# Sliding-window attention and soft mixture of experts on one core: second-layer weight chunks of one expert, eight 128-column transposes, row sums in two parts, ten row blocks stored by column halves

## Chip, core and metric

The kernel runs on one core of one Trainium2 chip. The metric is device time in microseconds (us); smaller is better. A core has TensorE (PE, with its weight loads shown as PEld), VectorE (DVE), ScalarE (ACT), GpSimd (POOL), SyncE (SP) and 16 DMA engines.

## The reference

The input is q, k and v of shape (8, 8, 576, 64) in fp32, a router phi (512 x 32) and the weights of eight experts, w1 (8 x 512 x 1024) and w2 (8 x 1024 x 512). The output is 4608 x 512 in fp32.

```python
scores = scale * q @ k.T            # heads 0-3: window of 32; heads 4-7: 128, every fourth
x = softmax(masked scores) @ v      # (4608, 512) after the heads are put side by side
logits = x @ phi                    # 32 slots, 4 of each expert
d = softmax of logits over the rows (axis 0)
slot_input = (d.T @ x).reshape(8, 4, 512)
for e in range(8):
    slot_out[e] = np.maximum(slot_input[e] @ w1[e], 0.0) @ w2[e]
c = softmax of logits over the slots (axis 1)
out = c @ slot_out
```

## The kernel before

The program is written as operations with engine, cost and key. A planner (`Prog.schedule`) puts them in order by estimated due times, and `emit` writes each engine's list with its semaphore waits. POOL and SP operations keep the order in which they are written. Where the planner sees a gap on TensorE within `FILL`, it inserts matmuls of the identity that nobody reads (`filler`, L1014); the function `keep` (L910) puts in `WARM` more of them after part p2 below.

The first 130 us are eight units of attention. POOL loads each unit's q, v and k with a cast to bf16 into one of three parts of `stg`; TensorE transposes (L574, L579), makes scores (L617) and weighted values (L671); the logits are made in `expT` (L726, L731) and the slots' inputs accumulate (L774). The weights follow in the same POOL queue, cast to bf16 on the way: w1 of experts 0 to 6 into `WD`, then "w17" and the second-layer weights. Their order in the queue is w17, p3a, p0, p1, p2, p3b, p3c, p3d, p3e. A number in such a name is a pair of experts g, so p0 is w2 of experts 0 and 1, and pair 3 is cut into five parts by chunk and, for the last four, by column half. One chunk is 128 rows of w2, of both experts: in `(e p) c f` partitions 0 to 63 hold expert 2g and partitions 64 to 127 hold expert 2g + 1, sixteen chunks in all. p0 goes in 13 transfers, some of them small dummies into `scr` (`TURNS`)[...].

From 132 us on comes the tail, to which the change belongs:

1. The slots' inputs are transposed (`fold`, L827) into `siT`, and layer 1 runs (L846). ReLU puts the first half of the hidden values into `h_sb` on ACT (L854), the second on DVE (L857).
2. Because a chunk holds two experts, the hidden values are transposed with the selector `half` in two groups of 64 columns: 2 times 16 matmuls (L866). ACT and DVE copy the results into `hT` (L875), one instruction each.
3. Layer 2 multiplies `hT` with the chunks of p3a, p0, p1 (L894), then TensorE sums the 36 columns of the combine weights (L921; DVE's reciprocal at L926 gives `rtok`), then come p2, the `WARM` matmuls, p3b and p3c. With p3b and p3c the first 256 columns of the slots' outputs are complete, and DVE scales them into `so_sb` (L935). p3d and p3e give the other 256 columns.
4. The output is made in seven groups of row blocks of 128 rows, `TILES` with 1, 2, 3, 5, 4, 8 and 13 blocks. The first `NSPLIT` = 4 groups, eleven blocks, are made in two column halves: the first half (rows of 1 KB) while p3d and p3e are still on their way, the second after them. The last three groups, 25 blocks, are made with full rows. TensorE multiplies (L972), and DVE (L983 for two blocks of 256 columns at once, L991 for one) or ACT (L989) scales by `rtok` into a staging place that the weights no longer need (`STAGE`). SP stores each group, or half of a group, with one transfer (L1005) when it is complete.

Of the kernel before, what the change touches and what calls it, by code (L numbers as in the profile page):

```python
# [23 lines left out]
FILL = (118,141)  # L24
# [293 lines left out]
def bass_dilated_sliding_attn__then__soft_moe_slots_kernel(  # L318
# [14 lines left out]
    def sb(name, shape, dt=BF16):  # L333
        return A(nc.sbuf_tensor(name, shape, dt))

    WARM = 7
    TURNS = ((32, 0, 4), (32, 1, 4), (32, 2, 4), (16, 3, 8), (15, None, 0), (6, 39, 8), (2, None, 0),
             (2, 87, 8), (6, None, 0), (4, 103, 8), (2, 7, 8), (2, None, 0), (2, 23, 8))
    W2 = {"p3a": (3, 0, 4, 0, 512), "p0": (0, 0, 16, 0, 512), "p1": (1, 0, 16, 0, 512),
          "p2": (2, 0, 16, 0, 512), "p3b": (3, 4, 14, 0, 256), "p3c": (3, 14, 16, 0, 256),  # L340
          "p3d": (3, 4, 14, 256, 512), "p3e": (3, 14, 16, 256, 512)}
# [27 lines left out]
    half = sb("half", [128, 2, 32])  # L369
# [40 lines left out]
    b_psA, b_csum, b_rcs, b_rtok = [Buf() for _ in range(4)]  # L410
# [35 lines left out]
    def wload(name):  # L446
# [3 lines left out]
        if name[:2] == "w1":  # L450
            src = moe_w1[int(name[2:])].rearrange("(p c) f -> p c f", c=4)
            dst = ap.rearrange("p (c f) -> p c f", c=4)
        else:
            g, c0, c1, f0, f1 = W2[name]
            src = moe_w2[2 * g:2 * g + 2].rearrange("e (p c) f -> (e p) c f", c=16)[:, c0:c1, f0:f1]
            dst = ap.rearrange("p (c f) -> p c f", f=f1 - f0)
        if name == "p0":
            src = src.rearrange("p (x c) f -> p x (c f)", x=2)
            dst = ap.rearrange("p (x y) -> p x y", x=2)[:, :, 0:4096]

            def skewed(g):
                res = []
                for i, (n, r, step) in enumerate(TURNS):
                    if r is None:
                        res.append(g.dma_start(scr[0:n, i], src[0:n, :, 0:8]))
                    else:
                        e = r + step * (n - 1) + 1
                        res.append(g.dma_start(dst[r:e:step], src[r:e:step]))
                return res
            op("pool", skewed, after=b.prev, a=[b], cost=0.6 * (len(TURNS)), sem=sem, nbytes=512 * 8192,  # L470
               nd=288, nq=len(TURNS))
            return
# [6 lines left out]
    home(stg[:, 2, 4096:6144], [b_stg[2]], "p3a")  # L479
    home(stg[:, 2, 6144:8704], [b_stg[2]], "p3b")  # L480
# [52 lines left out]
    for x in range(2):  # L533
        for j in range(4):
            op("dve", lambda g, x=x, j=j: g.tensor_copy(
                half[32 * j:32 * j + 32, x, 8 * j + 4 * x:8 * j + 4 * x + 4],
                ident[32 * j:32 * j + 32, 32 * j + 4 * x:32 * j + 4 * x + 4]),
               r=[b_id], w=[b_half], cost=0.1, key=1)
# [321 lines left out]
    for p_ in range(2):  # L860
        ht = tile(psum, 1)

        def pe(t, p_=p_, ht=ht):
            for c in range(8):
                for x in range(2):
                    i_ = t.matmul(bank(ht)[64 * x:64 * x + 64, 32 * c:32 * c + 32],  # L866
                                  h_sb[:, 8 * p_ + c::16], half[:, x, :], start=True, stop=True)
            return i_
        op("pe", pe, r=[b_h[0], b_h[1], b_half], w=[ht], alloc=[ht], cost=0.95, mode="h",
                 key=K1, ni=32)  # L870

        def ev(en, p_=p_, ht=ht):
            d_ = hT[:, 8 * p_:8 * p_ + 8, :].rearrange("p c (j i) -> p c j i", j=4)[:, :, :, 0:8]
            s_ = bank(ht)[:, 0:256].rearrange("p (c j i) -> p c j i", c=8, j=4)
            return en.activation(d_, s_, ACTF.Copy) if p_ == 0 else en.tensor_copy(d_, s_)  # L875
        op("act" if p_ == 0 else "dve", ev, r=[ht], w=[b_hT[p_]], cost=0.35, key=K1)

    TILES = []
    NSPLIT = 4
    POOLS = False  # L880
    for n in (1, 2, 3, 5, 4, 8, 13):
# [5 lines left out]
    for k_, name in enumerate(W2):  # L887
        g, c0, c1, f0, f1 = W2[name]
        wv = HOME[name][0].rearrange("p (c f) -> p c f", f=f1 - f0)
        for h_ in range(f0 // 256, f1 // 256):  # L890
            def pe(t, k_=k_, name=name, g=g, c0=c0, c1=c1, h_=h_, wv=wv, f0=f0):
                for c in range(c0, c1):
# [3 lines left out]
                                  wv[:, c - c0 + (name == "p0" and c > 7), 256 * h_ - f0:256 * h_ - f0 + 256],  # L896
                                  start=(k_ == 0 and c < 4), stop=(k_ > 3 and c >= 12))
                return i_
            last_ = op("pe", pe, r=b_hT + [HOME[name][1]], alloc=[sp_] if k_ == h_ == 0 else [],
                       a=[sp_, b_sp[h_]], cost=0.13 * (c1 - c0) / 4, mode="c",  # L900
                       ni=2 * (c1 - c0),
                       key=K1 + 2 + 0.5 * k_ + 0.1 * h_ + (28 if k_ > 5 else 0))
            if k_ == 2:
                mid = last_
# [11 lines left out]
    rs = tile(psum, 1)  # L916

    def rsum(t):
        for o, (_, n) in enumerate(TILES):
            for j in range(n):  # L920
                i_ = t.matmul(bank(rs)[:, rcol[o] + j:rcol[o] + j + 1], tok[o][j], rowm[:],  # L921
                              start=True, stop=True)
        return i_
    op("pe", rsum, r=b_expT + [b_rowm], w=[rs], alloc=[rs], cost=2.0, key=K1 + 3, ni=72,
       after=[mid])
    op("dve", lambda vv: vv.reciprocal(rtok[:], bank(rs)[:, 0:N_TOK // 128]), r=[rs], w=[b_rtok],  # L926
       cost=0.2, key=K1 + 1)

# [10 lines left out]
    for o_ in P.ops[-2:]:  # L939
# [6 lines left out]
    STAGE = [(w17f[:, 0:512], ["w17"]), (w17f[:, 512:1536], ["w17"]), (p0f[:, 0:1536], ["p0"]),  # L946
             (p0f[:, 1536:4096], ["p0"]), (p1f[:, 0:2048], ["p1"]), (WDf[:, 6656:10752], wdh),
             (WDf[:, 0:6656], wdh)]
    nev = 0
    for o, h_ in [(o, h_) for h_ in range(2) for o in range(NSPLIT)] + [(o, None) for o in range(NSPLIT, 7)]:  # L950
        t0, n = TILES[o]
        ost = STAGE[o][0].rearrange("p (j f) -> p j f", j=n)
        sl = slice(0, 512) if h_ is None else slice(256 * h_, 256 * h_ + 256)
        ob = Buf()
        for x in STAGE[o][1]:
            ob.prev = ob.prev + HOME[x][1].ready + HOME[x][1].reads
        k1 = K1 + 30 + o + 10 * (2 if h_ is None else h_)
        w = sl.stop - sl.start
        for j0 in range(0, n, 2):
            po = tile(psum, w // 256)  # L960
            kk = k1 + 0.1 * j0
            b_po = [Buf(), Buf()]

            def slot(j, po=po, w=w):
                if w == 512:
                    return pair(po)[:, j, :]
                return bank(po)[:, w * j:w * j + w]
            m = min(2, n - j0)
            for js in [range(m)] if w == 256 else [(j,) for j in range(m)]:
                def pe(t, o=o, slot=slot, j0=j0, js=js, sl=sl):  # L970
                    for j in js:
                        i_ = t.matmul(slot(j), tok[o][j0 + j], so_sb[:, sl], start=True, stop=True,  # L972
                                      skip_group_check=True)
                    return i_
                j = js[0]
                p0 = op("pe", pe, r=(b_so if h_ is None else b_so[h_:h_ + 1]) + b_expT, a=[po],
                        w=[b_po[j]], alloc=[po] if j == 0 else [], after=[p0] if j else [],
                        cost=0.22 if h_ is None else 0.15 * m, key=kk + 0.01 * j, ni=2 * len(js))
                col = rcol[o] + j0 + j

                def ev(en, slot=slot, ost=ost, js=js, j0=j0, sl=sl, col=col, po=po):
                    if en is nc.vector and len(js) == 2:
                        return en.tensor_tensor(  # L983
                            ost[:, j0:j0 + 2, sl], bank(po).rearrange("p (j f) -> p j f", j=2),
                            rtok[:, col:col + 2].unsqueeze(2).to_broadcast([128, 2, 256]), AluOp.mult)
                    for j in js:
                        d_, s_, sc_ = ost[:, j0 + j, sl], slot(j), rtok[:, col + j - js[0]:col + j - js[0] + 1]
                        if en is nc.scalar:
                            i_ = en.activation(d_, s_, ACTF.Copy, scale=sc_)  # L989
                        else:  # L990
                            i_ = en.tensor_scalar(d_, s_, sc_, None, op0=AluOp.mult)  # L991
                    return i_
                if w == 256:
                    o_ = op(("dve", "act"), ev, r=[b_po[j], b_rtok], a=[ob], after=ob.prev,
                            cost={"dve": 0.7 if m == 2 else 0.48, "act": 0.47 * m}, key=kk)
                else:
                    o_ = op(("dve", "act")[nev % 2], ev, r=[b_po[j], b_rtok], a=[ob], after=ob.prev,
                            cost=0.66, key=kk)
                    nev += 1
                o_.touch.append(po)  # L1000
                po.left += 1
        so = DmaSem(nc, f"s_out{o}_{h_}")
        s_out.append(so)
        op("pool" if POOLS and h_ is not None and (h_ or o > 1) else "sp",
           lambda e, t0=t0, n=n, ost=ost, sl=sl: [e.dma_start(  # L1005
               out[t0:t0 + 128 * n, sl].rearrange("(p j) f -> p j f", j=n), ost[:, :, sl])],
           r=[ob], cost=0.1, sem=so, nbytes=512 * n * w, key=k1)
# [60 lines left out]
```

## Time and profile before

| what | value |
|---|---|
| median of five runs | 179.17 us (177.8 to 181.73) |
| the profiled execution | 178.26 us, its span 176.5 us |
| mean granted TensorE clock | 0.927 of full |
| busy: PE, DVE, ACT, POOL | 133.1, 113.4, 95.7, 43.5 us |
| POOL's queue (loads with cast) | 30.94 MB, 87.1% of 16 engines' span |
| SP's queue (output) | 9.50 MB, 13.8% |
| HBM read, written | 61.93 MB, 9.44 MB: 404 GB/s over the span |

The page cuts the span into 40 slices of 4.4 us; a digit is a busy share in tenths. A transfer's bytes are counted on the side that it writes, so loads that turn fp32 into bf16 count half of what they read. Busy time of an engine says little here: what counts is which wait ends last in a stage.

### The profile page before, as it was taken

How to read it: one execution, taken by the hardware profiler on the slowest of the kernel's cores; microseconds unless marked ns; L12 is line 12 of the kernel's file. 1: busy time of each engine (PE TensorE's matmuls, PEld its weight loads, DVE VectorE, ACT ScalarE, POOL GpSimd, SP SyncE). 2: the span in 40 equal slices, each digit the busy share in tenths (PEclk: the TensorE clock that was granted, in tenths of full speed). 3: DMA queues.
4: the chain of work that ended last, by engine and by line, in shares of the span. 5: the costliest groups of instructions: out<-in, count | busy, mean ns of one | idle time of the engine just before them, and what ended most of it. 6: DMA issues, size and time to landing. Idle time of an engine off the chain costs nothing.

```text
span 176.5 us, 5828 instructions
## 1 busy us (share of the span) xinstructions
PE 133.1 (75%) x2619; PEld 105.1 (60%) x2619; DVE 113.4 (64%) x259; ACT 95.7 (54%) x144; POOL 43.5 (25%) x83
## 2 busy tenths in 40 slices
PE   0009798695999877999949999986999998695000
PEld 0009587584897676898848978874646685441000
DVE  6850388965887984898974699899550102899000
ACT  2004889584895963878944689686310100797000
POOL 7991707007004302600100690106100000000000
PEclk9999999997899998899995799999999999999655
DMA  5999999999999999999999999999999999799996
GB/s 82 190 215 211 213 217 213 214 217 212 220 213 210 217 219 207 216 219 213 212 215 214 217 213 216 214 219 212 230 200 219 230 166 196 224 341 402 458 440 290
DMA packets 11672, 40.80 MB, mean 231 GB/s; under 512 B 2176, under 2 KB 8064, under 8 KB 8192
## 3 DMA queue, kind: packets, MB, share of 16 engines
q0 software_dynamic: 7744, 30.94, 87.1%
q1 hardware_dynamic: 3904, 9.50, 13.8%
q8 instruction: 20, 0.33, 0.7%
q14 instruction: 4, 0.03, 0.0%
HBM read 61.93 MB, written 9.44 MB: 404 GB/s over the span
## 4 chain that ended last, share of the span: by engine, by line
PE 37%; DMA 21%; DVE 20%; issue 6%; ACT 5%; POOL 3%; POOLq 1%; DVEq 0%
DMA TT<-in_moe_w_dram 16%; PE ps L579 9%; PE ps L574 6%; DMA stg<-in_k_dram 5%; DVE PT L632 5%; PE ps L671 4%; PE ps L642 4%; PE ps L617 4%; DVE WD L991 4%; DVE XB L682 4%; PE ps L726 4%; DVE VN L647 4%; PE ps L699 3%; ACT TT L599 2%; ACT PT L624 2%
## 5 line engine op out<-in xcount | busy, mean ns | idle before, releaser
L624 ACT ACTIVATE PT<-ps 128x768 bf16<-128x768 f32 x48 | 37.0, 816 | 11.1 <-PE ps L617 10.7
L599 ACT ACTIVATE TT<-ps 128x864 f32<-128x864 f32 x32 | 28.6, 896 | 20.1 <-PE ps L579 17.2
L682 DVE TENSOR_TENSOR XB<-ps,RV 96x768 bf16<-96x768 f32 x32 | 30.4, 951 | 0.9
L579 PE MATMUL ps<-ident,stg 96*64 96x96 bf16 x576 | 18.7, 232 | 14.4 <-DMA stg<-in_k_dram 12.9
L579 PEld LDWEIGHTS ps<-ident,stg 96*64 96x64 bf16 x576 | 16.7, 129 | 15.7 <-DMA stg<-in_k_dram 12.9
L647 DVE COPY VN<-ps 128x768 bf16<-128x768 bf16 x32 | 17.1, 543 | 12.0 <-PE ps L642 11.9
L617 PE MATMUL ps<-TT 64*128 64x96 bf16 x384 | 16.3, 211 | 6.5 <-issue 4.2
L671 PE MATMUL ps<-VN,PT 128*128 128x65 bf16 x384 | 18.7, 198 | 3.2 <-issue 2.0
L430 POOL DMA_DIRECT2D stg<-in_q_dram x16 | 8.8, 549 | 42.4 <-PE ps L579 23.7
L671 PEld LDWEIGHTS ps<-VN,PT 128*128 128x128 bf16 x384 | 15.4, 101 | 4.5 <-issue 2.1
L642 PE MATMUL ps<-ident,TT 128*128 128x128 bf16 x192 | 17.2, 234 | 0.6 <-ACT PT L624 0.3
L617 PEld LDWEIGHTS ps<-TT 64*128 64x128 bf16 x384 | 10.2, 97 | 10.4 <-issue 4.5
L712 ACT ACTIVATE XT<-ps 128x576 bf16<-128x576 bf16 x22 | 13.7, 652 | 3.8 <-PE ps L699 3.8
L574 PE MATMUL ps<-ident,stg 96*128 96x96 bf16 x288 | 14.7, 206 | 0.4 <-DVE XB L682 0.4
L699 PE MATMUL ps<-ident,XB 96*128 96x96 bf16 x192 | 13.6, 218 | 0.9 <-DVE XB L682 0.9
L574 PEld LDWEIGHTS ps<-ident,stg 96*128 96x128 bf16 x288 | 13.2, 98 | 1.3 <-DVE XB L682 0.5
L642 PEld LDWEIGHTS ps<-ident,TT 128*128 128x128 bf16 x192 | 12.2, 104 | 2.9 <-DVE VN L647 0.6
L632 DVE TENSOR_TENSOR PT<-PT,mask_d 128x768 bf16<-128x768 bf16 x24 | 12.9, 545 | 1.1 <-ACT PT L624 1.0
L632 DVE TENSOR_TENSOR PT<-PT,mask_p 128x768 bf16<-128x768 bf16 x24 | 12.8, 551 | 1.0 <-ACT PT L624 0.6
L699 PEld LDWEIGHTS ps<-ident,XB 96*128 96x128 bf16 x192 | 10.5, 106 | 2.3 <-DVE XB L682 1.2
L972 PE MATMUL ps<-so_sb,expT 128*128 128x512 bf16 (+1 forms) x47 | 9.6, 334 | 1.9 <-DVE so_sb L935 1.2
L989 ACT ACTIVATE stg<-ps,rtok 128x256 f32<-128x256 f32 (+1 forms) x12 | 5.1, 512 | 10.6 <-PE ps L972 10.6
(83 smaller groups left out, 184.6 us busy)
## 6 DMA issues: line engine op xcount, KB each, us to landing
WD<-in_moe_w_dram POOLq DMA_DIRECT2D x7, 1024.0 KB, 30.6
stg<-in_q_dram POOLq DMA_DIRECT2D x16, 288.0 KB, 20.3
stg<-in_v_dram POOLq DMA_DIRECT2D x16, 288.0 KB, 21.1
stg<-in_k_dram POOLq DMA_DIRECT2D x16, 288.0 KB, 22.2
out_dram<-WD SPq DMA_DIRECT2D x1, 3328.0 KB, 12.4
stg<-in_moe_w_dram POOLq DMA_DIRECT2D x4, 512.0 KB, 20.4
stg<-in_moe_w_dram POOLq DMA_DIRECT2D x1, 2048.0 KB, 21.9
TT<-in_moe_w_dram POOLq DMA_DIRECT2D x1, 2048.0 KB, 23.2
```

The lines of the kernel that those rows point to most:

```text
L574: i_ = t.transpose(bankb2(pt, a)[:, 96 * kk:96 * kk + 96], two[:, j // 2, c, :], ident[0:96, 0:96])
L579: i_ = t.transpose(bankb2(pt, a)[64 * hx:64 * hx + 64, 96 * kk:96 * kk + 96], src[:, hx, c, :], ident[0:96, 0:96])
L599: return ac.activation(d, sv, ACTF.Copy)
L617: i_ = t.matmul(pair(sc)[:, hx, QB * x:QB * x + QB], win(u, 1, h01, blk_, bpar)[64 * hx:64 * hx + 64], win(u, 0, h01, blk_, bpar)[64 * hx: ...
L624: op("act", lambda ac: ac.activation(sbt(pt)[:, 0:768].rearrange("p (x n) -> p x n", x=2), pair(sc)[:, :, 0:384], ACTF.Exp, scale=SCALE), ...
L632: return dv.tensor_tensor(p_, p_, m.unsqueeze(1).to_broadcast([128, 2, 384]), AluOp.mult)
L642: i_ = t.transpose(bankb(pv)[:, 128 * m:128 * m + 128], win(u, 2, h01, m, bpar), ident[:, :])
L647: op("dve", lambda dv: dv.tensor_copy(sbt(vn)[:, :, :, 0:64], bankb(pv)[:, 0:768].rearrange("p (m x d) -> p m x d", m=6, x=2)), r=[pv], w= ...
L671: i_ = t.matmul(pair(po)[:, bk, 65 * po_:65 * po_ + 65], sbt(pts[i])[:, o_:o_ + 128], sbt(vn)[:, m, half, 0:65], start=True, stop=True)
L682: op("dve", lambda dv: dv.tensor_tensor(sbt(xb)[:].rearrange("p m (x h d) -> p h x m d", x=2, h=2)[:, h01], pv()[:, :, :, 0:64], sbt(rv)[: ...
L699: i_ = t.transpose(bankb(px)[:, QB * m:QB * m + QB], sbt(xb)[:, m, 128 * x:128 * x + 128], ident[0:QB, 0:QB])
L712: return en.activation(d, s_, ACTF.Copy)
```

## The change

- A chunk of second-layer weights now holds 128 rows of one expert: chunks 0 to 7 belong to expert 2g and 8 to 15 to expert 2g + 1. A partition reads two runs of 16 KB, one from each expert, where it read one of 32 KB. `half` has 16 columns for each of the two slot sets instead of 32, and 8 matmuls of 128 weight columns stand in place of the 32 transposes. The copies into `hT` have two instructions each.
- p3a has chunks 0 to 5 (0 to 3 before), p3b and p3d have chunks 6 to 13 (4 to 13 before). p3b and p3d go in two transfers each, since their chunks come from two experts.
- The row sums and their reciprocals are in two parts: 10 columns after layer 1, 26 after p1.
- `TILES` is 1, 1, 2, 3, 3, 4, 8, 14 and `NSPLIT` is 5: ten blocks by column halves, 26 with full rows. The blocks of the first groups are taken in the units 1, 1, 2, 2, 2, 2, also across the border of two groups. DVE evicts two blocks with two instructions instead of one (L983 goes).
- `WARM` is 8 instead of 7, and `FILL` ends at 138 instead of 141 of the planner's time. In the order that results, the four filling matmuls just ahead of the transposes give way to the ten row sums. Ahead of that place every engine's order is the same as before.

```diff
-FILL = (118,141)
+FILL = (118,138)
-    WARM = 7
+    WARM = 8
-    W2 = {"p3a": (3, 0, 4, 0, 512), "p0": (0, 0, 16, 0, 512), "p1": (1, 0, 16, 0, 512),
-          "p2": (2, 0, 16, 0, 512), "p3b": (3, 4, 14, 0, 256), "p3c": (3, 14, 16, 0, 256),
-          "p3d": (3, 4, 14, 256, 512), "p3e": (3, 14, 16, 256, 512)}
+    W2 = {"p3a": (3, 0, 6, 0, 512), "p0": (0, 0, 16, 0, 512), "p1": (1, 0, 16, 0, 512),
+          "p2": (2, 0, 16, 0, 512), "p3b": (3, 6, 14, 0, 256), "p3c": (3, 14, 16, 0, 256),
+          "p3d": (3, 6, 14, 256, 512), "p3e": (3, 14, 16, 256, 512)}
...
-            src = moe_w2[2 * g:2 * g + 2].rearrange("e (p c) f -> (e p) c f", c=16)[:, c0:c1, f0:f1]
-            dst = ap.rearrange("p (c f) -> p c f", f=f1 - f0)
+            src = moe_w2[2 * g:2 * g + 2].rearrange("e (p c) f -> e p c f", c=8)
+            dst = ap.rearrange("p (c f) -> p c f", f=f1 - f0) if name != "p0" else None
+            if c1 - c0 < 16:
+                def rows(gp):
+                    res = []
+                    for x in range(2):
+                        lo, hi = max(c0, 8 * x), min(c1, 8 * x + 8)
+                        if lo < hi:
+                            res.append(gp.dma_start(dst[:, lo - c0:hi - c0, :],
+                                                    src[x][:, lo - 8 * x:hi - 8 * x, f0:f1]))
+                    return res
...
+            src = src.rearrange("e p c f -> p e (c f)")
+            dst = ap.rearrange("p (x y) -> p x y", x=2)[:, :, 0:4096]
...
-            for c in range(8):
-                for x in range(2):
-                    i_ = t.matmul(bank(ht)[64 * x:64 * x + 64, 32 * c:32 * c + 32],
-                                  h_sb[:, 8 * p_ + c::16], half[:, x, :], start=True, stop=True)
+            for c in range(4):
+                i_ = t.matmul(bank(ht)[:, 32 * c:32 * c + 32], h_sb[:, 4 * p_ + c::8],
+                              half[:].rearrange("p x i -> p (x i)"), start=True, stop=True)
...
-    NSPLIT = 4
-    POOLS = False
-    for n in (1, 2, 3, 5, 4, 8, 13):
+    NSPLIT = 5
+    for n in (1, 1, 2, 3, 3, 4, 8, 14):
...
+    row_sums(0, [ffn1])
+    row_sums(1, [mid])
+
+    def scaled(en, d_, s_, c):
+        if en is nc.scalar:
+            return en.activation(d_, s_, ACTF.Copy, scale=rtok[:, c:c + 1])
+        return en.tensor_scalar(d_, s_, rtok[:, c:c + 1], None, op0=AluOp.mult)
...
+        for us in [units[0:1], units[1:2]] + [units[i:i + 2] for i in range(2, len(units), 2)]:
...
-                    if en is nc.vector and len(js) == 2:
-                        return en.tensor_tensor(
-                            ost[:, j0:j0 + 2, sl], bank(po).rearrange("p (j f) -> p j f", j=2),
-                            rtok[:, col:col + 2].unsqueeze(2).to_broadcast([128, 2, 256]), AluOp.mult)
```

The other lines of the diff carry this through: the column sums' buffers `b_rt`, the function `store` with SP's transfers, and the staging places `STAGE` for eight groups.

## The prediction

> **What bounds the kernel now.** I read the page's rows by slice first. The DMA share stands at 9 from the second slice to the end, with one dip. The granted clock is full from 99.7 us to 164.5 us, and the matmul rows are empty after 161.6 us. So the span is a transfer time: weights and inputs in, then 9.44 MB of output out.
>
> ```profile
> span 176.5 us, 5828 instructions
> ...
> DMA  5999999999999999999999999999999999799996
> ```
>
> Next I cut the last 35 us into windows of one transfer kind each (columns: busy us of PE, PE loads, DVE, ACT, POOL, then clock, DMA share, GB/s; an in-transfer counts its bf16 side, so 215 GB/s is 430 read).
>
> ```profile
> 104.00:109.00 5.00, 5.00 (x114) 4.65 (x112) 4.60 (x12) 4.17 (x8) 1.99 (x4) 1.00 1.01 211
> 134.00:141.00 7.00, 7.00 (x103) 3.96 (x103) 0.98 (x2) 0.98 (x2) 0.00 (x0) 1.00 1.02 218
> 142.00:149.00 7.00, 6.87 (x159) 5.09 (x151) 0.44 (x2) 0.00 (x0) 0.00 (x0) 1.00 1.41 193
> 149.60:151.10 1.50, 1.36 (x15) 1.05 (x17) 1.29 (x3) 1.07 (x3) 0.00 (x0) 1.00 0.78 100
> 151.10:152.10 1.00, 0.70 (x12) 0.22 (x11) 0.83 (x3) 0.86 (x3) 0.00 (x0) 1.00 0.41 135
> 152.10:153.10 1.00, 0.47 (x5) 0.43 (x6) 0.62 (x2) 0.00 (x0) 0.00 (x0) 1.00 0.96 321
> 153.00:159.00 6.00, 5.50 (x28) 2.81 (x25) 6.00 (x11) 5.83 (x12) 0.00 (x0) 1.00 1.01 340
> ```
>
> The reader is to see the one hole, from 149.6 to 153 us, between the last weights (p3d, p3e) and an output stream that runs without a break from 153 us on. Weighing 149.6 to 151.1 against the 1.41 share of small-row loads and the rest against 1.0, the hole is worth 0.67 + 0.59 + 0.04 = 1.3 us. Outside it the end can move only if bytes become cheaper.
>
> What opens the hole is read from the timeline and the store issues:
>
> ```profile
> 139.05 2.10 PE L866 MATMUL ps<-half,h_sb 128*64 128x32 bf16 x32
> 143.91 1.91 PE L921 MATMUL ps<-rowm,expT 128*128 128x1 bf16 x36
> 146.74 1.69 PE L910 MATMUL ps<-mask_p,ident 128*128 128x512 bf16 x7
> 148.35 0.51 PE L894 MATMUL ps<-stg,hT 128*32 128x256 bf16 x10
> 148.95 0.48 DVE L935 TENSOR_SCALAR so_sb<-ps,rcs 128x256 bf16<-128x256 f32 x1 [2.71 <-PE ps L894]
> ...
> 150.32 0.35 SPq L1005 DMA_DIRECT2D out_dram<-stg  x1
> 150.89 0.61 SPq L1005 DMA_DIRECT2D out_dram<-stg  x1
> 151.62 0.54 SPq L1005 DMA_DIRECT2D out_dram<-stg  x1
> 152.26 0.59 SPq L1005 DMA_DIRECT2D out_dram<-stg  x1
> ```
>
> Landings are issue plus the issue table's time: p2 120.49 + 23.2 = 143.7, p3b 121.03 + 26.0 = 147.0, p3c 121.99 + 25.7 = 147.7, p3d 151.0, p3e 151.7 us. So p3c was in at 147.7, but TensorE reached p3b only at 148.35, when its seven warming matmuls ended: the first half is 0.65 us late for TensorE's own reasons. The second half waits for nothing but p3e:
>
> ```profile
> 123.64 28.07 DMA TT<-in_moe_w_dram
> 151.72 0.04 issue
> 151.76 0.30 PE ps L894 x2
> ```
>
> **The change, part by part.**
>
> *Transposes.* 32 (L866) took 2.10 us, a pitch of 63 ns. No row has the new shape. The nearest are the 36 row sums, also with 128-column strided weights: 1.91/36 = 53 ns. Bounds 53 and 100 ns (a 128x128 load in L574 lasts 98, if none overlapped); I take 60, close to the nearest row: 8 x 60 = 0.5 us, 1.6 us less. Each eviction becomes two pieces of 64 elements for one of 256 (383 ns ACT, 425 ns DVE). The shortest row like it, 128x128 cast, is 291 ns; two pieces cost 0.4 to 0.58, I take 0.5. The DVE one now starts at about 139.7 and ends at 140.2 instead of 141.6 us, so hT is ready 1.4 us sooner.
>
> *Row sums.* 10 columns go into the wait for the DVE's relu (TensorE only filled there, 138.08 to 139.04): 0.53 us, hidden; without cover it would delay the transposes by that. 26 stay after p1, 1.4 us for 1.9.
>
> *Weights.* p3a grows from 4 to 6 chunks of 512 columns and heads the queue of p0, p1, p2; p3b and p3d shrink from 10 to 8. p2 (16 such chunks) followed p1 (landed 112.04 + 21.9 = 133.9) by 9.8 us, 0.61 per chunk, so p2 lands 1.2 us later, at 144.9. Ten quarter-size chunks of p3d took 151.0 - 147.7 = 3.3 us, 0.33 each. Four fewer small ones save 1.32 and cost 1.22: p3e gains 0.1. Against that, p1 and p2 go in 8 KB packets from two experts for 16 KB ones; w1 is loaded in 8 KB packets: 211 against 218 GB/s above. Over 5 us this ratio is rough, because whole packets are counted at their end; the packet records have 605 ns for 8 KB and 1,227 for 16 KB, equal per byte. Ends: -0.1 and +0.6 us (3% of the 19.5 us of p1 and p2); I take +0.1, by the packet times. Two more POOL issues (0.6 to 1.0 us each) end near 126 us, 16 us before their data moves. So p3e stays at 151.7; p3c, with two small chunks fewer behind it, lands at 148.3.
>
> Here a rule speaks against the change. The Trainium skill, *DMA: Bandwidth & Descriptors*, section "Latency and other measured facts", gives copies whose row pitch is a large power of two as slow: 207 GB/s at 512 KiB and 164 at 2 MiB, where full is 214. The two runs of a partition now lie one expert apart, 1024 x 512 x 4 B = 2 MiB. By the rule's worst figure p0, p1 and p2, some 29 us, would take 214/164, 8.8 us more. The row says otherwise: before, half of the partitions already read the one expert and half the other in the same transfer, and it is the fastest window (218). I take no loss, and keep the rule's milder end (3%, 1 us) for a rival.
>
> *TensorE after that.* Layer-2 parts p3a, p0, p1: 76 matmuls at the 30 ns of L894 (2.15/72) from 140.4 to 142.7; 26 row sums to 144.1; wait for p2 (144.9) and its 32 to 146.0; eight warming matmuls at 0.24 (1.69/7) to 147.9; p3b (landed 147.7) to 148.2; p3c at 148.35. Before, p3e's landing led to so_sb in 0.37 us, so so_sb starts at 148.7 instead of 148.95: **0.27 us sooner, of the 1.6 saved**. The rest is swallowed by p2 and p3c. What is late next is p3c.
>
> *First stores.* Tile 1 has one block, not two, so its store can go when ACT is done (480 ns) and SP free: issues at about 150.05, 150.45 instead of 150.32, 150.89, and 0.35 us long instead of 0.61. Packets start 0.8 us after a small issue: the second store's data follow the first's without the gap that 151.1 to 152.1 shows. Against this DVE evicts pairs in two instructions, 2 x 0.44 for 0.60 (L983 starts at 150.25 and 150.85): the third store can't leave before 150.9, the fourth 151.8; a gap of 0.3 to 0.4 us stays. Counting blocks out by 154.25 (0.38 us each), I get 7.4 for 6.7: 0.27 us gained; ends 0 and 0.9 (the hole nearly shut). Later DVE is no bound: after 20 half blocks and 26 full ones it ends at 163.8, as before (163.6), 4 us ahead of the stream.
>
> *Ten rows by columns instead of eleven.* One block goes out once at 2 KB a row, not twice at 1 KB. The last store's 13 blocks took (163.66 + 12.4) - (159.10 + 9.1) = 7.9 us, 0.605 each; ten half blocks of the second half landed from 156.9 to 160.8, 0.38 to 0.39 each. Saved 2 x 0.385 - 0.605 = 0.16 us. Two more stores cost SP 0.7 us, beside a full queue.
>
> *Clock.* The Trainium skill, *TensorE: Matmul & The Clock Gate*, section "Why this matters for your kernels", wants no idle gap above about 3 us. The trace is stricter: 3.41 us windows with 1.52 and 1.19 us of matmul were followed by half clock, 1.97 and 2.17 were not. The rule lets the new gaps (1 us at most) pass; by the row they are near the edge, as the tail's windows fall from 2.17 to about 2.0. If it trips, pairs cost 0.87 instead of 0.66 us for one window: 0.9 us, hidden by the same 4 us.
>
> **Sum:** -0.27 - 0.16 = **-0.4 us**. The profiled execution took 178.26 us (1.76 around its span): 177.85. The median of the runs is 179.17, 0.5% above it; on that scale 178.7.
>
> **Rivals.**
> 1. *Hidden anyway*: the store pipeline sets the hole; an earlier first half leaves the same gaps. For: stores are issued one after another. Against: the second issue waited for ACT. Only the cheaper rows count: -0.16, 179.0 us. Chance 0.17.
> 2. *The hole shuts*: -0.9 - 0.16: 178.1 us. Against: the slower DVE pair. Chance 0.1.
> 3. *Slower: the two-expert reads of p0, p1 and p2.* Place: 113 to 144 us. At 3% 29 us become 30, so +0.9 - 0.3 = +0.6, 179.8; at the rule's 2 MiB figure +8.4, 187.6. It decides from 1.5% (0.4 us). Against: the 218 window. Chance 0.13.
> 4. *p2 arrives too late for the warming matmuls.* From 0.65 us later than reckoned the first half starts later than now: +0.2, 179.4. Chance 0.08.
>
> The forecast has 0.52. About 1% is what a measurement here can tell, since the five runs shown spread over 2%. All but the strong end of rival 3 lie inside that; with the spread of medians I give 0.11 faster, 0.76 within, 0.13 slower. The range takes in rival 2 with a low median (177.2) and rival 3's mild end with a high one (180.7).
>
> **What would show it.** Right: transposes near 0.5 us, so_sb's first half near 148.7, p3e still near 151.7, a second store within 0.5 us of the first, last store issued near 163.9. Wrong: p3e after 152.3 (rival 3), warming matmuls ending after p3c lands (rival 4), or an unbroken DMA share from 151 us (rival 2).

## The result: 0.46% slower, where 0.2% faster was forecast

| | before | changed |
|---|---|---|
| median of all runs | 178.88 us (80 runs) | 178.98 us (43 runs) |
| lower and upper quartile | 177.72, 179.96 | 178.66, 179.60 |
| fastest run | 176.94 | 177.62 |
| ratio, 95% interval | | 1.0046 (1.0027 to 1.0065) |
| span of the profiled execution | 176.5 | 176.9 |

The ratio compares the runs of each kernel within 1.5% of its fastest, which leaves out 27 of the 80 runs of before and 5 of the 43 of the changed kernel. The medians of all runs differ by 0.1 us only. The quartiles say why: the change raises the lower quartile by 0.9 us and takes 0.4 us from the upper one.

The page of the changed kernel, rows by slice, and below them the clock row of before:

```profile
span 176.9 us, 5780 instructions
...
PEclk9999999997899998799996999999999987999655
DMA  5999999999999999999999999999999999699997
```

```profile
PEclk9999999997899998899995799999999999999655
```

Two things are new in the tail. The DMA dip in the sixth slice from the end is deeper (6 for 7), and the granted clock falls in slices 33 and 34 (8, 7), ahead of that dip. Cut as before, the hole reads (columns as in the prediction):

```profile
149.60:151.10 1.50, 1.01 (x10) 0.93 (x10) 1.12 (x3) 0.58 (x2) 0.00 (x0) 1.00 0.66 85
151.10:152.10 1.00, 0.72 (x13) 0.22 (x10) 1.00 (x4) 1.00 (x4) 0.00 (x0) 1.00 0.32 109
152.10:153.10 1.00, 0.19 (x2) 0.18 (x3) 0.75 (x2) 0.42 (x2) 0.00 (x0) 1.00 0.50 167
```

By the prediction's weighing it is 0.80 + 0.68 + 0.50 = 2.0 us, where 1.3 were lost before and 1.0 expected. The timeline of the same execution says why (line 908 is layer 2, 925 the warming matmuls, 937 so_sb):

```profile
140.88 1.62 PE L977 MATMUL ps<-rowm,expT 128*128 128x1 bf16 x26
142.54 0.32 DVE L981 RECIPROCAL rtok<-ps 128x26 f32<-128x26 f32 x1 [4.14 <-PE ps L977]
144.83 1.90 PE L908 MATMUL ps<-TT,hT 128*32 128x256 bf16 x32 [2.33 <-DMA TT<-in_moe_w_dram]
146.66 2.41 PE L925 MATMUL ps<-mask_p,ident 128*128 128x512 bf16 x8
149.00 0.40 PE L908 MATMUL ps<-stg,hT 128*32 128x256 bf16 x8
149.54 0.48 DVE L937 TENSOR_SCALAR so_sb<-ps,rcs 128x256 bf16<-128x256 f32 x1 [6.68 <-PE ps L908]
```

TensorE comes to p2 early and waits 2.33 us. p2's 32 matmuls then take 1.90 us and the eight warming ones 2.41, where 1.06 and 1.89 to 1.90 are their times at full clock (a_warm and a_pad below). p3b starts at 149.0, with p3c in since 148.1, and so_sb at 149.54 instead of the forecast 148.7. The windows view, cut at the clock's own steps, shows the cause:

```profile
140.91:144.32 3.41, 1.59 (x28) 1.51 (x26) 0.32 (x1) 0.00 (x0) 0.00 (x0) 1.00 1.04 192
144.32:147.73 3.41, 2.90 (x35) 1.51 (x36) 0.00 (x0) 0.00 (x0) 0.00 (x0) 0.50 1.44 194
```

A window with 1.59 us of matmul (first number after its length) is followed by one at clock 0.50 (the third number from the end). The chain of waits no longer goes from p3e into the output, but from p2:

```profile
118.88 25.91 DMA TT<-in_moe_w_dram
144.83 1.90 PE ps L908 x16
146.72 2.34 PE ps L925 x8
150.41 2.05 DVE stg L990 x5
```

**One number carries every profile.** Span minus the start of so_sb's first half is 27.6 us in before and in both variants of it that keep its groups of rows. With the new groups it is 27.3 to 27.4 in twelve of fourteen profiles. The other two, a_w3 and a_w1, read 27.8 and 27.9, explained below. So I read each experiment by the start of so_sb, and by what held it. I call an execution early or late by when TensorE starts the transposes of the hidden values: at 137.3 us in this profile, at 139.05 in that of before.

### The profile page after: what moved, and what is told of

It reads as the page before. It is cut to its first block, busy times and chain, and to the rows that moved or that the text cites. A ratio compares the mean times of both kernels' runs of the same rounds, so it can differ in the third digit from the quotient of the medians.

```text
span 176.9 us, 5780 instructions
## 1 busy us (share of the span) xinstructions
PE 131.9 (75%) x2591; PEld 102.6 (58%) x2591; DVE 113.2 (64%) x263; ACT 96.4 (55%) x146; POOL 45.1 (25%) x85
## 4 chain that ended last, share of the span: by engine, by line
PE 42%; DMA 20%; DVE 19%; issue 5%; ACT 5%; POOL 1%; DVEq 0%; POOLq 0%
DMA TT<-in_moe_w_dram 15%; PE ps L591 9%; PE ps L586 6%; PE ps L683 5%; DMA stg<-in_k_dram 5%; PE ps L629 5%; PE ps L654 5%; DVE WD L990 4%; PE ps L738 4%; PE ps L711 4%; DVE PT L644 3%; DVE XB L694 3%; DVE stg L990 3%; DVE VN L659 3%; ACT PT L636 2%
## 5 line engine op out<-in xcount | busy, mean ns | idle before, releaser
L692 DVE RECIPROCAL RV<-ps 96x12 f32<-96x12 f32 x32 | 7.1, 223 | 4.2 <-PE ps L683 4.0
```

## The experiments

Theory C: the wait for p2 halves the clock, which stretches p2 and the warming matmuls. Theory F: with 48 fewer instructions and slow transposes gone, TensorE reaches the next 16 KB piece of its own program before it has been fetched. Rival P: the new cut lands p3c 0.5 us later. Rival D: DVE's two instructions for a pair. "so_sb" is the start of its first half.

Each ratio is to runs of before made alongside. Their median was 178.88 us beside the changed kernel and 177.8 to 178.1 beside the variants. a_pair, which differs from the changed kernel in DVE's pairs alone, measured 1.0048 in that company, so the loss shows there too.

| run | edit | ratio (95% interval) | so_sb, us | span, us |
|---|---|---|---|---|
| a_fill | nine matmuls ahead of p2 | 1.0031 (1.0000 to 1.0062) | 152.5 | 179.9 |
| a_pair | pairs in one DVE instruction | 1.0048 (1.0020 to 1.0076) | 149.5 | 176.8 |
| a_cut | old cut of pair 3 | 1.0020 (0.9975 to 1.0064) | 149.8 | 177.1 |
| b_tiles | before, new groups only | 0.9995 (0.9963 to 1.0027) | 147.8 | 175.1 |
| a_pad | program shifted by 23 matmuls | 1.0001 (0.9967 to 1.0034) | 148.6 | 175.9 |
| a_warm | warming matmuls ahead of p2 | 0.9990 (0.9964 to 1.0016) | 148.7 | 176.1 |
| b_tr | before, new chunks and transposes only | 1.0021 (0.9975 to 1.0067) | 147.7 | 175.3 |
| b_cut | before, new cut only | 1.0052 (1.0014 to 1.0090) | 148.3 | 175.9 |
| a_cutpad | a_cut, program shifted by 27 | 1.0003 (0.9971 to 1.0036) | 148.7 | 176.0 |
| a_best | a_cutpad, WARM 5 | 0.9983 (0.9957 to 1.0008) | 148.5 | 175.8 |
| a_w3 | WARM 3 | 1.0010 (0.9981 to 1.0039) | 148.3 | 176.1 |
| b_w4t | b_tiles, WARM 4 | 0.9992 (0.9961 to 1.0023) | 149.7 | 177.0 |
| a_w1 | a_cutpad, WARM 1 | 0.9989 (0.9963 to 1.0014) | 147.9 | 175.8 |
| after2, after3 | the changed kernel again | one run each | 149.7, 149.6 | 177.0, 176.9 |

**a_fill**, work for TensorE in the wait:

```diff
     row_sums(1, [mid])
...
+        for _ in range(9):
...
+    op("pe", keep2, r=[b_id, b_mask[0]], w=[hold], alloc=[hold], cost=0.216 * 9,
+       ni=18, key=K1 + 2.8, after=[P.ops[-2]])
```

> The changed kernel plus nine matmuls of the identity that nobody reads, between the 26 row sums and p2, where TensorE stood idle for 2.3 us in its profile. Theory C (the idle time cools the clock, the eight warming matmuls then run at half speed and hold p3b back to 149.0 us): clock full through 142 to 152 us, warming matmuls 1.7 to 1.9 us instead of 2.4, so_sb's first half at about 148.5 to 148.8, ratio to before 0.996 to 1.000. Rival P (the first half is late because p3c lands 0.5 us later in the stream, whatever the clock): ratio stays at 1.003 to 1.006. Rival D (DVE's two instructions for a pair delay the second half): ratio stays at 1.003 to 1.006 and the second so_sb still starts 0.9 us after p3e lands.

The ratio fell only to 1.0031. The runs divide: ten of 22 are at 177.3 to 178.0 us, eight at 179.0 or more. The profile is one of the late ones (transposes at 142.1), in which p2 ran without stop or half clock, but nine more matmuls stood in the way. The ten runs at the low end would fit C for early executions, but no profile shows one, and the late ones pay. It doesn't decide.

**a_pair**, DVE's pairs:

```diff
+                if en is nc.vector and len(us) == 2:
...
+                    return en.tensor_tensor(
+                        d_, bank(po).rearrange("p (j f) -> p j f", j=2),
+                        rtok[:, c:c + 2].unsqueeze(2).to_broadcast([128, 2, 256]), AluOp.mult)
```

> The changed kernel with DVE evicting a pair of half blocks in one instruction, as before the change, also across the border of groups 4 and 5. Rival D: the second so_sb starts within 0.45 us of p3e's landing (0.9 in the changed kernel), the third and fourth stores go out 0.3 us sooner, ratio 1.000 to 1.003. Theory C and rival P: ratio stays at 1.003 to 1.006, since the first half starts as late as in the changed kernel.

The second so_sb started 0.71 us after p3e's landing (0.89 in the changed kernel; D expected under 0.45). The third and fourth stores went out 2.24 and 2.97 us after so_sb, where the changed kernel has 2.25 and 2.98: in both SP is still issuing the second store when the third could go. Neither the ratio nor the 27.3 moved, and D falls. This profile brought something new. Its clock was full from 125.7 us on, and yet TensorE stood still inside p2 (timeline):

```profile
144.88 0.94 PE L908 MATMUL ps<-TT,hT 128*32 128x256 bf16 x25
146.76 0.40 PE L908 MATMUL ps<-TT,hT 128*32 128x256 bf16 x7 [0.94 <-issue]
```

**a_cut**, the old cut:

```diff
-    W2 = {"p3a": (3, 0, 6, 0, 512), ... "p3b": (3, 6, 14, 0, 256), ...
+    W2 = {"p3a": (3, 0, 4, 0, 512), ... "p3b": (3, 4, 14, 0, 256), ...
```

> The changed kernel with the old cut of pair 3: p3a four chunks, p3b and p3d ten. p2 lands 1.2 us sooner, p3c about 0.5 sooner, p3e 0.2 later. Theory C: the idle time before p2 shrinks to about 1.1 us, the clock stays full, so_sb's first half at about 148.1 to 148.4, ratio 0.995 to 0.999, about as a_fill or better by 0.2. Rival P: the gain is p3c's 0.5 us alone whatever the clock does, ratio 1.001 to 1.003. Rival D: 1.003 to 1.006.

p2 came 1.3 us sooner (143.5) and p3c at 147.5. so_sb started at 149.8 all the same, since TensorE stopped for 1.36 us after 29 matmuls of p2. Its timeline:

```profile
144.75 1.05 PE L908 MATMUL ps<-TT,hT 128*32 128x256 bf16 x29
147.16 0.29 PE L908 MATMUL ps<-TT,hT 128*32 128x256 bf16 x3 [1.36 <-issue]
```

This kernel has four matmuls, eight instructions with their weight loads, fewer ahead of p2, and the stop comes four matmuls later: it sits at one place of the program, not at one time. In the trace's packet records a 16,384-byte packet of the instruction queue ends 1.4 us before TensorE goes on, here (145.7 and 147.2) as in a_pair (145.4 and 146.8). That queue moved 20 such packets in the whole run, 0.33 MB, some 64 bytes for each of TensorE's matmuls and weight loads; so I take it to bring TensorE's program. This made theory F. The ratio is unclear.

**b_tiles**, only the groups of rows on the kernel before:

```diff
-    NSPLIT = 4
+    NSPLIT = 5
     POOLS = False
-    for n in (1, 2, 3, 5, 4, 8, 13):
+    for n in (1, 1, 2, 3, 3, 4, 8, 14):
...
```

> The kernel before with only the groups of row blocks of the changed one (1, 1, 2, 3, 3, 4, 8, 14; ten blocks by column halves). All theories: the cheaper rows save 0.16 us and the smaller second store up to 0.3, ratio 0.997 to 1.000. If the groups themselves are at fault (six one-block or two-block evictions on DVE, two more stores on SP): 1.001 to 1.004.

The ratio can't tell, but span minus so_sb is 27.3 for 27.6: the groups save 0.3 us. The profile is of an early execution, so_sb at 147.8, span 175.1: TensorE's work up to so_sb is that of before, so before can be 1.1 us earlier there than in the profile from which I predicted.

**a_pad**, the program border moved, nothing else:

```diff
+    def padding(t):
+        for _ in range(23):
+            i_ = t.matmul(bank(pd)[:, 0:1], ident[:, :], ident[:, 0:1], start=True, stop=True)
...
```

> The changed kernel plus 23 one-column matmuls that nobody reads, in the first 12 us where TensorE has nothing to do. They move every later instruction of TensorE 46 places back in its program, so that the place in p2 where TensorE stood still for 0.9 and 1.4 us in the profiles of a_pair and a_cut comes to p2's first matmul, about where it was before the change. Theory F (TensorE now reaches the next 16 KB piece of its own program before that is fetched; an instruction fetch packet ended 1.4 us ahead of the restart both times): no stop inside p2, ratio to before 0.998 to 1.002. Theory C (the 2.3 us of waiting for p2 halve the clock): no change of the ratio, 1.003 to 1.006, and where TensorE is early a wait of over 2 us before p2 followed by a half-clock stretch. Rival P (p3c lands 0.5 us later): 1.003 to 1.006, p3b without a late start.

1.0001 for 1.0046; the two intervals overlap a little (0.9967 to 1.0034 and 1.0027 to 1.0065). In its timeline p2 has no stop:

```profile
143.69 1.62 PE L984 MATMUL ps<-rowm,expT 128*128 128x1 bf16 x26
145.24 1.06 PE L915 MATMUL ps<-TT,hT 128*32 128x256 bf16 x32
146.23 1.90 PE L932 MATMUL ps<-mask_p,ident 128*128 128x512 bf16 x8
148.61 0.48 DVE L944 TENSOR_SCALAR so_sb<-ps,rcs 128x256 bf16<-128x256 f32 x1 [2.94 <-PE ps L915]
```

TensorE was as late here as in a_pair (transposes at 140.1 and 139.8), and so_sb is 0.9 us earlier. The 16 KB packet that ended at 145.4 us in a_pair has its counterpart at 142.2. 23 useless matmuls at the start take out the stop: that is what F expects and the other theories do not.

The packet records also show what such a packet follows. In the seven profiles of the changed kernel and of its variants with the new cut and no padding it starts 4.3 to 4.6 us after the transposes, though these start anywhere from 137.3 to 142.1 us. So it follows TensorE's own place in the program. An early TensorE does not outrun it, but stands waiting for p2 when it comes; a late one, for which p2 has landed, runs into the stop.

One thing doesn't fit theory C as the main loss. a_pad leaves the wait for p2 as it was, so its early executions should still lose to the clock. It has four of 22 runs at 178.1 to 178.7 us, where the changed kernel's two profiles with half clock lie, and ten at 177.3 to 177.6, where the changed kernel has one of 43. These run times suggest that the stop is the more frequent loss; no profile shows it.

**a_warm**, the eight warming matmuls ahead of p2:

```diff
-        if k_ == 3:
+        if k_ == 2:
...
-               ni=2 * WARM, key=K1 + 3.9, after=[last_])
+               ni=2 * WARM, key=K1 + 2.8, after=[last_])
```

> The changed kernel with its eight warming matmuls ahead of p2 instead of behind it; the number of instructions stays. They then fill the wait for p2, and give a fetch 1.7 us more time. Theories F and C both: p3b starts with its landing, so_sb's first half at 148.3 to 148.7, clock full to 149 us, ratio 0.996 to 1.000. Rival P: the same start of so_sb, but ratio 1.002 to 1.005, since p3c's landing is what costs. If neither the clock nor the fetch is at fault, the warming matmuls are missed after p2 and the clock falls in 148 to 152: 1.003 to 1.008.

As F and C expected: so_sb at 148.74 although TensorE was late, full clock, no stop.

```profile
145.49 1.89 PE L925 MATMUL ps<-mask_p,ident 128*128 128x512 bf16 x8
147.31 1.06 PE L908 MATMUL ps<-TT,hT 128*32 128x256 bf16 x32
148.74 0.48 DVE L937 TENSOR_SCALAR so_sb<-ps,rcs 128x256 bf16<-128x256 f32 x1 [2.75 <-PE ps L908]
```

All 22 runs lie between 177.34 and 178.07 us, where the changed kernel's lie between 177.6 and 182.6. From this narrow spread I take it that one move takes away both losses; the profile is of a late execution and shows it for the stop alone. What stays is in the main p3c's landing (148.1): the fastest run is 0.5 us above the fastest of before (176.82).

**b_tr**, chunks of one expert and eight transposes, on the kernel before:

```diff
-            for c in range(8):
-                for x in range(2):
-                    i_ = t.matmul(bank(ht)[64 * x:64 * x + 64, 32 * c:32 * c + 32],
-                                  h_sb[:, 8 * p_ + c::16], half[:, x, :], start=True, stop=True)
+            for c in range(4):
+                i_ = t.matmul(bank(ht)[:, 32 * c:32 * c + 32], h_sb[:, 4 * p_ + c::8],
+                              half[:].rearrange("p x i -> p (x i)"), start=True, stop=True)
...
```

> The kernel before with only the chunks of one expert and the eight transposes; the cut of pair 3, the groups of rows, the row sums and WARM stay as before. p2 lands as before. Theory F: 48 fewer instructions bring a stop of 0.5 to 1.4 us into p2 or the wait behind it, ratio 1.000 to 1.004, transposes' 1.5 us lost. Theory C alone: the wait for p2 is 0.5 us or less, the clock stays, ratio 0.996 to 0.999. Rival P: 0.996 to 0.999, the cost is in the cut.

The stop is there too, 0.47 us after the 25th matmul of p2, but in an early execution, which p3c's landing (147.3) held anyway. The ratio is unclear. p2, p3c and p3e landed at 143.3, 147.3 and 151.5, against 143.7, 147.7 and 151.7 before: reading two experts cost the transfers nothing here.

**b_cut**, only the new cut on the kernel before (a_cut's edit the other way round):

```diff
-    W2 = {"p3a": (3, 0, 4, 0, 512), ... "p3b": (3, 4, 14, 0, 256), ...
+    W2 = {"p3a": (3, 0, 6, 0, 512), ... "p3b": (3, 6, 14, 0, 256), ...
```

> The kernel before with only the cut of pair 3 changed: p3a six chunks, p3b and p3d eight, in the old layout. p2 lands 1.2 us and p3c 0.5 us later. Rival P: the first half starts at 148.5 to 148.9 at the best, ratio 1.002 to 1.005. Theories F and C: with the slow transposes TensorE comes to p2 about when it lands, no stop and no half clock; only executions in which TensorE is early lose up to 0.5 us: ratio 1.000 to 1.002.

Rival P fits this part: 1.0052, with an interval that is clear of 1 but reaches down to what F and C allowed (1.000 to 1.002). p3c landed at 147.97 and so_sb followed it (timeline, line 894 layer 2):

```profile
147.35 0.40 PE L894 MATMUL ps<-stg,hT 128*32 128x256 bf16 x8
148.01 0.29 PE L894 MATMUL ps<-TT,hT 128*32 128x256 bf16 x2 [0.26 <-DMA TT<-in_moe_w_dram]
148.34 0.48 DVE L935 TENSOR_SCALAR so_sb<-ps,rcs 128x256 bf16<-128x256 f32 x1 [3.52 <-PE ps L894]
```

**a_cutpad**, both undone together (a_cut's edit, and a_pad's with 27 for 23), **a_best** and **a_w1**, the same with 5 and 1 warming matmuls:

```diff
-    WARM = 8
+    WARM = 5
```

> The changed kernel with the old cut of pair 3 (p3a four chunks) and 27 one-column matmuls in the first 12 us, which bring the piece border of TensorE's program to p2's first matmul. In all profiles so far the span is the start of so_sb's first half plus 27.3 us with the new groups (27.6 with the old). If fetch and cut are two separate costs: no stop in p2, p3c in at 147.4, so_sb at 147.8 to 148.6 according to how late TensorE arrives, ratio to before 0.995 to 0.999, some 0.3 us below a_pad. If the cut costs nothing of its own: as a_pad, 0.999 to 1.001.

> As a_cutpad, with 5 warming matmuls instead of 8. If the warming matmuls, whose time is fixed, are what holds p3b back where TensorE arrives late: so_sb at 147.8 to 148.0 in nearly all executions, ratio 0.992 to 0.997. If the clock needs them: half clock behind p2 in part of the executions, ratio 0.997 to 1.003.

> As a_best, with 1 warming matmul instead of 5. If half clock costs nothing by itself at this place (a_best had it from 151.0 to 154.4 us and its span was still so_sb plus 27.3), only its lengthening of p2 and of the warming matmuls: so_sb follows p3c's landing in all executions, 147.8 to 148.2, ratio 0.993 to 0.998, narrower than a_best. If the first output matmuls need the clock: 0.999 to 1.005.

a_cutpad's ratio is where I expected it if the cut costs nothing of its own (0.999 to 1.001). Only its fastest runs show the cut: they are at 176.9 us, where a_pad's are at 177.3. Its median is about that of a_pad (177.97 and 178.05). In its profile, of a late execution, so_sb started at 148.7 though p3c was in at 147.5: the warming matmuls held it. With 5 the times draw together (three quarters of the runs within 177.74 us, before within 179.0 in that comparison) and the ratio is 0.9983, with 1 it is 0.9989; neither is clear of 1, and neither reaches what I expected if the warming matmuls only stood in the way (0.992 to 0.998). a_w1 has half clock from 150.7 to 157.5 us, and there span minus so_sb is 27.9. From 155 to 157 us its DMA share is 0.74, where a_best has 1.02: the output matmuls pay about 0.6 us for the clock. In a_best a half-clock window from 151.0 to 154.4 cost nothing.

**a_w3**, WARM 3 in the changed kernel, and **b_w4t**, WARM 4 for 7 in b_tiles:

```diff
-    WARM = 8
+    WARM = 3
```

> The changed kernel with 3 warming matmuls instead of 8, nothing else. The stop in p2 or the half clock stays, but 1.1 us of what stands behind it goes: so_sb at 148.4 to 148.6, ratio 0.997 to 1.001. If the clock then falls for the first output matmuls: 1.002 to 1.008.

> The kernel before with the new groups of rows and 4 warming matmuls instead of 7, slow transposes and old cut. In executions where TensorE is late, p3b starts 0.65 us sooner; in the others p3c's landing sets it: so_sb at 147.7 to 148.3, ratio 0.993 to 0.998. If the warming matmuls are needed: 0.999 to 1.005.

a_w3 stopped for 0.70 us in p2 and still had so_sb at 148.3. Its second store took SP 0.93 us to issue instead of 0.43, which is as much as the 27.8 has over 27.3. b_w4t's profile is of a late execution (transposes at 140.5), its ratio unclear and above the 0.993 to 0.998 that I expected; half of its runs are within 177.3.

**after2, after3**, the changed kernel again:

> The changed kernel once more, for a second profile. If the stop for instructions is the usual loss: with TensorE at the hidden transposes after 138.5 us, a stop of 0.4 to 1.4 us after the 25th matmul of p2; with TensorE there before 138 us, a wait of over 1 us for p2 instead. If the half clock is the usual one: half clock somewhere in 142 to 149 us and no stop.

> The changed kernel a third time, as after2: stop after the 25th matmul of p2 (fetch), or half clock in 142 to 149 us (clock).

Both losses are there, one in each. In after2 TensorE was late (transposes at 140.3):

```profile
145.38 0.94 PE L908 MATMUL ps<-TT,hT 128*32 128x256 bf16 x25
147.00 0.40 PE L908 MATMUL ps<-TT,hT 128*32 128x256 bf16 x7 [0.68 <-issue]
147.56 1.67 PE L925 MATMUL ps<-mask_p,ident 128*128 128x512 bf16 x7 [0.16 <-issue]
```

In after3 it was early (137.4), waited 2.0 us for p2, and the windows read

```profile
142.61:146.02 3.41, 1.29 (x34) 0.98 (x36) 0.32 (x1) 0.00 (x0) 0.00 (x0) 0.99 1.28 183
146.02:149.44 3.42, 3.42 (x17) 1.04 (x15) 0.00 (x0) 0.00 (x0) 0.00 (x0) 0.51 1.45 197
```

so that its warming matmuls took 3.0 us. so_sb starts at 149.7 and 149.6, and at 149.5 in the first profile: late by the stop or late by the clock, the changed kernel is at the same place. How often each happens isn't known from three profiles.

## Why the prediction was wrong

*What bounds the kernel*: right in kind. The end follows the start of so_sb one for one. But "the first half is 0.65 us late for TensorE's own reasons" was true of that execution. In b_tiles and b_tr, whose TensorE is no faster to that point or only by the transposes, so_sb starts at 147.8 and 147.7: in b_tr p3c's landing (147.3) holds it, in b_tiles the warming matmuls end at 147.2, just as p3c lands (147.3). The executions differ by when TensorE arrives at the transposes of the hidden values (137.2 to 142.1 us over all profiles), and I took one arrival for all. What makes it early or late was not looked into.

*Transposes and row sums*: 0.67 us for eight transposes (0.5 forecast) and 1.62 for 26 row sums (1.4), hT ready as reckoned; the 1.5 us were saved and then all lost.

*Weights*: p2 at 144.8 (144.9), p3c at 148.1 (148.3), p3e at 151.5 (151.7): right. Leaving the 2 MiB rule aside was right too, no loss (the rule speaks of the pitch from one partition to the next, and here the 2 MiB lie within a partition). The packet time was misread: 8 KB take 625 ns in the records, not 605, 2% more per byte than the 16 KB packets; p2's landing shows nothing of it. But I let p3c's 0.5 us be paid by a TensorE that was late. Where it isn't, the cut costs its full size (b_cut, 1.0052), though by the ratios of a_cutpad and a_pad it costs nothing; that stays open.

*TensorE after that* is the step that failed. "26 row sums to 144.1; wait for p2 (144.9) and its 32 to 146.0; eight warming matmuls ... to 147.9" had p2 run straight through at full clock, and put nothing, ahead of so_sb, for TensorE's own program or for the wait's effect on the clock. It took a stop of 0.7 us at its 25th matmul in after2, and in the other two half clock: p2's 32 took 1.90 us for 1.06 and the warming ones 2.41 for 1.9 in the first profile, 1.35 us together. The gain of 0.27 us at so_sb became a loss of 0.6.

*Clock*: "the new gaps (1 us at most)" were 2.3 and 2.0 us; an early TensorE adds to the 1.5 us saved. I put the price on the output matmuls, where a_best shows it hidden; it fell on p2 and the warming matmuls, ahead of so_sb. The two windows before it, 1.59 and 1.29 us of matmul, are on the side of the prediction's 1.52; but its border between 1.52 and 1.97 does not hold in the other profiles (last section).

*First stores and rows*: the second store went 0.39 us after the first (150.92, 151.31), and the last at 163.92, as forecast. Apart from so_sb's start the groups save 0.3 us (27.6 to 27.3), where the sum had 0.16 for the cheaper rows; its 0.27 for the first stores took the earlier so_sb and the quicker second store together. a_pair shows DVE's pairs to cost nothing.

The sum against the profile of before: +0.59 at so_sb, -0.27 for the groups, +0.32 us of span. Rival 4 named the mark, warming matmuls ending after p3c lands, but not the cause: p2 was not late.

## What to carry over

A saving on an engine is worth what the next arrival allows: before counting it, ask what that engine will wait for, whether the wait cools its clock, and whether its own program is there to be run. When executions of one kernel scatter by more than the change is worth, find what moves between them before reading one profile's slack as a property of the kernel. Here idle work put in to hold a clock did better ahead of the wait than behind it: a_warm moved eight matmuls and the scatter shrank to 0.7 us.

## What the chip showed that I had not expected

- A program is itself a transfer. With the DMA queues full, TensorE went on 1.3 to 1.4 us after the 16 KB packet of its program had ended, in five profiles with a stop, and the stop moved with the instruction count. The packet starts a nearly fixed time after TensorE's own transposes; when the piece is asked for, no record shows, so how long its fetch takes stays open.
- 23 one-column matmuls in the idle start took the stop out of p2, and with them the kernel measured level with before (1.0001).
- How much matmul time in a window of 3.41 us keeps the clock has no sharp border in these traces. Windows with 1.59 us and less, where the text shows them, were followed by half clock. But so was one with 2.35 (b_w4t, 92.18 to 95.59 us), while one with 1.77 kept full clock (b_tiles, 147.91 to 151.33).
